# Value products alone in their PSUM banks, global scores in one bank, and new orders of loads, of ScalarE and of the end, in an attention and soft-MoE kernel

## Chip, cores and metric
One core of one Trainium2 chip, all data fp32 (the mask constants are bf16). The time is device microseconds of one execution. The change is judged by the ratio of the times of the two kernels.

## Reference
Attention over 8 batches and 8 heads with 512 local and 32 global tokens, head size 64. A local query sees the 32 global keys and the local keys at a distance of at most 32; a global query sees all 544. The result is a matrix of 4608 tokens x 512, which goes through a soft mixture of 8 experts with 4 slots each:

```python
s_g = scale * np.matmul(q_g, k_all.transpose(0, 1, 3, 2))
out_g = np.matmul(sm(s_g), v_all)
s_ll = np.where(mask, scale * np.matmul(q_l, k_l.transpose(0, 1, 3, 2)), -1000000000.0)
s_lg = scale * np.matmul(q_l, k_g.transpose(0, 1, 3, 2))
out_l = np.matmul(sm(np.concatenate([s_lg, s_ll], axis=-1)), np.concatenate([v_g, v_l], axis=2))
...
logits = x @ phi                          # 4608 x 512 by 512 x 32
d = softmax of logits over the tokens;  slot_input = d.T @ x
h = np.maximum(slot_input[e] @ w1[e], 0.0);  slot_out[e] = h @ w2[e]
c = softmax of logits over the slots;   return c @ slot_out
```

## The kernel before, in words
The attention runs in 32 steps s, one for two heads of one batch: b = s // 4, q = s % 4. Two steps, an even and an odd one, are a pair i = s // 2; the global queries of a pair are worked on together.

What one step does, engine by engine. TensorE forms the masked scores of the next step in tile pS (`scores`, 72 products); VectorE takes their maximum (L242) and subtracts it into the step's tile w (L244); TensorE turns w into pT (`turn_pair`, L120); ScalarE takes the exponentials of pT (L251); TensorE forms the value products of the step before in pO (`values`); VectorE normalises them into x (`normalise`, L286 to L288). GpSimd copies v into two shifted forms (L260 to L263).

Even steps also form the global scores of the pair: `global_small` in pT and `global_main` in both halves of pM, pM0 and pM1, one row half of 64 in each. ScalarE copies them to sgr in four copies of 64 partitions (L302, L312). VectorE takes the maximum gm (L319), GpSimd subtracts it into sgs (L322). TensorE turns sgs into columns of pO behind the value products (from column GOFF on), a part in the odd step (`turn_global(0)`) and a part in the next even step; ScalarE takes their exponentials into eg (L343). `global_values` forms the global outputs in pM1, and VectorE and GpSimd scale and place them (L360 to L366).

At odd steps the x of two steps is turned into both halves of pM and copied out as xT (L388). At q = 2 the logits of the batch before are formed in pM0, at q = 3 their running soft maximum follows (`soft`), the weights dT are turned into columns of pO and copied as dd (L349), and at q = 0 `sums` adds the weighted tokens to acc. Logits of the global tokens have a column of their own and extra steps (18 to 23).

Every engine runs its instructions in the order in which the code states them. SP issues all loads in the order of the list `queue` (L170): "k" is a load of q and k of a step (kq, 624 KB, 3 buffers), "v" its values (390 KB, 5 buffers), "p" a page of 512 KB of the experts' weights. `pump` paces a load by making it wait for a product of TensorE; `allowed` holds it back in the code until the step that frees its buffer has been written.

After the last step the logits of the last batch, the slot inputs and their sums follow. Then `first_product` (w1) of two groups of experts, each followed by `hidden` (relu and turning on TensorE and ScalarE), `combine_weights` for three groups of tokens (soft maximum over the slots on VectorE, L680 to L686), `second_product` (w2) for two halves of the columns, and `combine` for 9 groups of tokens per half, with copies to ob by VectorE (L725) and ScalarE (L726) and the DMA of the result.

PSUM is four tiles of two banks, pS, pT, pO and pM, for the whole program.

Of the kernel before, what the change touches and what calls it, by code (L numbers as in the profile page):

```python
# [7 lines left out]
F32 = mybir.dt.float32  # L8
# [25 lines left out]
GOFF = 4 * VD  # L34
# [24 lines left out]
def kernel(ctx, tc, kq, vS, phi, w1, w2, cst, cbf, out):  # L59
# [24 lines left out]
    lT = keep.tile([P, 9, P], F32, name="lT")  # L84
    acc = keep.tile([P, DM], F32, tag="acc", name="acc")
    xgs = [keep.tile([P, DM], F32, tag=f"xg{i}", name=f"xg{i}") for i in range(2)]
    mrun = keep.tile([P, 1], F32, name="mrun")
    lrun = keep.tile([P, 1], F32, name="lrun")
    wrm = keep.tile([P, 256], BF16, name="wrm")
    dT = keep.tile([P, P], F32, name="dT")  # L90
    dTg = keep.tile([P, P], F32, name="dTg")
    dd = keep.tile([P, P], F32, name="dd")
    ddg = keep.tile([P, 2 * NS], F32, name="ddg")
# [172 lines left out]
    xs = {}  # L266
# [12 lines left out]

    def normalise(s):  # L280
        b, p = s // 4, s % 4
        if p == 0:
            xs[b] = xp.tile([P, 4, DM], F32, tag="x", name=f"x{b}")
        r = xp.tile([P, 8], F32, tag="r", name=f"r{s}")
# [9 lines left out]
    def global_small(i):  # L294
        for pp in range(2):
            k = kqs[2 * i + pp]
            for h in range(2):
                o = pT[64 * h + 32 * pp:64 * h + 32 * pp + 32, h, 0:64]
                for n, sl in ((0, GCOPY), (1, 5)):
                    mm(o[:, 32 * n:32 * n + 32], k[HALF[h], SQG, :], k[HALF[h], sl, :])  # L300
        for h in range(2):
            nc.scalar.copy(at_cols(sgr, HALF[h], 96, [(384, 2), (1, 32)]),  # L302
                           pT[HALF[h], h, 0:64].rearrange("p (a j) -> p a j", a=2))

    def global_main(i):
        for pp in range(2):
            k = kqs[2 * i + pp]
            for h in range(2):
                o = (pM0, pM1)[h][64 * h + 32 * pp:64 * h + 32 * pp + 32, 0:480]
                mm(o, k[HALF[h], SQG, :], at_cols(k, HALF[h], 0, [(192, 3), (32, 5), (1, 32)]))  # L310
        for h in range(2):
            nc.scalar.copy(at_cols(sgr, HALF[h], 0, [(32, 3), (P, 5), (1, 32)]),  # L312
                           (pM0, pM1)[h][HALF[h], 0:480].rearrange("p (r m j) -> p r m j", r=3, m=5))
# [3 lines left out]
    def global_max(i):  # L317
        gm[i] = xp.tile([P, 1], F32, tag="gm", name=f"gm{i}")
        nc.vector.reduce_max(gm[i], sgr, axis=AX.X)  # L319

    def global_shift(i):
        nc.gpsimd.tensor_scalar(sgs, sgr, gm[i], None, ALU.subtract)  # L322

    def turn_global(n):
        a, b = [], []
        for u, m in enumerate((0, 1, 2) if n == 0 else (3, 5)):
            lo, w = (P * m, 96 if m == 3 else P) if m < 4 else (480, P)
            src = sgs[:, lo:lo + w]
# [3 lines left out]
        return a, b  # L332

    def spare(u, n, w=P):

        return pO[0:w, :, GOFF + 64 * u:GOFF + 64 * (u + n)].rearrange("p r (u q) -> p u r q", q=64)

    def split(ap):
        return ap.rearrange("p u (r q) -> p u r q", r=2)

    def exp_global(n):
        for m, u, k, w in (((0, 0, 3, P),) if n == 0 else ((3, 0, 1, 96), (4, 1, 1, P))):
            nc.scalar.activation(split(eg[0:w, m:m + k, :]), spare(u, k, w), AF.Exp, scale=SCALE)  # L343

    def turn_d(src):
        return turn(lambda rt: pO[:, rt, GOFF + P:GOFF + 192], src)

    def copy_d():
        nc.scalar.copy(split(dd.unsqueeze(1)), spare(2, 1))  # L349
# [483 lines left out]
```

## Time and profile before
| | |
|---|---|
| time, median of 3 runs | 441.36 us (437.74 to 445.11) |
| the profiled execution, its own time | 442.88 us |
| its span | 441.1 us |
| TensorE busy, matmul | 271.7 us (62%) |
| VectorE, ScalarE, GpSimd busy | 173.3, 111.8, 130.7 us |
| mean granted clock of TensorE | 0.79 |
| moved by DMA | 77.10 MB, mean 175 GB/s |

The granted clock is given as a share of 2.4 GHz, so that 0.50 is the lower of the two levels. The chain that ended last is the list of what held up the end, followed back from the last instruction. An engine that is idle away from this chain costs nothing.

### The profile page before, as it was taken

To read this page: it belongs to the slowest core of one execution; us is meant where nothing else is said; L and a number is where in the kernel's file an instruction comes from. 1 tells how busy PE (TensorE), PEld (TensorE's weight loads), DVE (VectorE), ACT (ScalarE), POOL (GpSimd) and SP (SyncE) were. 2 spreads that over 40 slices of the span, in tenths; PEclk is the share of its full clock that TensorE was granted. 3 is DMA by queue.
4 is the path that set the end of the run, shared out by engine and by line. 5 is a ranking of instruction groups with operands and counts; after the bars stand their busy time and mean duration, and the time that the engine had idled before them with its cause. 6 is when DMAs were issued, how large, how long until landed. Compare 5 with 4: busy or idle time off the path is not lost.

```text
span 441.1 us, 15926 instructions
## 1 busy us (share of the span) xinstructions
PE 271.7 (62%) x7283; PEld 183.8 (42%) x7283; DVE 173.3 (39%) x329; ACT 111.8 (25%) x253; POOL 130.7 (30%) x216
## 2 busy tenths in 40 slices
PE   6673854555574657376566646457657686477852
PEld 4553634443453544355444434346445332243320
DVE  2544625352435434343534326254552322413231
ACT  1322413321322222233322213133251201212231
POOL 2536334260436143414251315143540000000000
PEclk9858869695969677868776859597995699589955
DMA  7655463425445253535353154444434989404774
GB/s 279 228 195 181 146 249 124 166 60 216 120 181 198 91 175 114 175 113 182 108 170 93 53 174 155 180 155 173 145 147 135 400 317 393 186 2 157 247 241 166
DMA packets 27907, 77.10 MB, mean 175 GB/s; under 512 B 2368, under 2 KB 11456, under 8 KB 27840
## 3 DMA queue, kind: packets, MB, share of 16 engines
q1 hardware_dynamic: 27840, 76.08, 49.0%
q8 instruction: 57, 0.93, 0.8%
q14 instruction: 10, 0.08, 0.1%
HBM read 67.16 MB, written 8.91 MB: 172 GB/s over the span
## 4 chain that ended last, share of the span: by engine, by line
PE 41%; DMA 20%; DVE 13%; ACT 6%; issue 4%; SPq 2%; POOL 1%; DVEq 0%; ACTq 0%
DMA kq<-in_kq_dram 20%; PE pS L117 16%; PE pO L117 8%; PE pM L117 8%; PE pT L117 4%; PE pM L120 2%; DVE ob L725 2%; ACT eg L343 2%; DVE x L288 2%; PE pT L120 2%; DVE mx L242 1%; PE pO L120 1%; SPq L154 1%; DVE w L244 1%; ACT sgr L312 1%
## 5 line engine op out<-in xcount | busy, mean ns | idle before, releaser
L242 DVE TENSOR_REDUCE mx<-pS 128x8 f32<-128x1024 f32 x32 | 39.2, 1224 | 116.1 <-PE pS L117 115.8
L117 PE MATMUL pO<-v,w 128*32 128x65 f32 x768 | 42.0, 245 | 48.4 <-ACT eg L343 38.4
L322 POOL TENSOR_SCALAR sgs<-sgr,gm 128x608 f32<-128x608 f32 x16 | 28.9, 1805 | 120.3 <-DVE gm L319 111.3
L117 PEld LDWEIGHTS pO<-v,w 128*32 128x32 f32 x768 | 36.2, 124 | 53.1 <-ACT eg L343 41.9
L117 PE MATMUL pS<-kq 64*32 64x128 f32 x2048 | 51.5, 340 | 0.7 <-issue 0.5
L117 PE MATMUL pT<-kq 64*32 64x32 f32 x256 | 12.3, 223 | 61.1 <-DMA kq<-in_kq_dram 61.1
L117 PEld LDWEIGHTS pS<-kq 64*32 64x32 f32 x2048 | 45.9, 130 | 3.7 <-issue 1.4
L251 ACT ACTIVATE w<-pT 128x1024 f32<-128x1024 f32 x32 | 32.7, 1023 | 44.3 <-PE pO L120 38.2
L117 PE MATMUL pO<-va,w 128*32 128x65 f32 x768 | 42.0, 244 | 0.0
L117 PE MATMUL pO<-vb,w 128*32 128x65 f32 x512 | 41.2, 244 | 0.0
L260 POOL COPY va<-v 128x650 f32<-128x650 f32 x32 | 23.2, 726 | 56.3 <-issue 48.0
L244 DVE TENSOR_TENSOR w<-pS,mx 128x1024 f32<-128x1024 f32 x32 | 39.2, 1224 | 1.1
L117 PEld LDWEIGHTS pO<-va,w 128*32 128x32 f32 x768 | 36.2, 125 | 0.0
L117 PEld LDWEIGHTS pT<-kq 64*32 64x32 f32 x256 | 8.5, 129 | 66.4 <-DMA kq<-in_kq_dram 63.0
L117 PEld LDWEIGHTS pO<-vb,w 128*32 128x32 f32 x512 | 35.3, 125 | 0.0
L120 PE MATMUL pT<-con,w 64*128 64x64 f32 x512 | 31.7, 248 | 0.0
L312 ACT COPY sgr<-pM 64x480 f32<-64x480 f32 x32 | 17.7, 554 | 48.4 <-PE pM L117 48.1
L117 PE MATMUL pM<-kq 64*32 64x480 f32 x128 | 28.6, 891 | 0.0
L302 ACT COPY sgr<-pT 64x64 f32<-64x64 f32 x32 | 6.6, 207 | 82.8 <-PE pT L117 78.4
L120 PEld LDWEIGHTS pT<-con,w 64*128 64x128 f32 x512 | 27.1, 160 | 1.3 <-issue 1.3
L120 PEld LDWEIGHTS pO<-con,sgs 64*128 64x128 f32 (+1 forms) x160 | 16.5, 152 | 26.5 <-DVE mx L242 15.4
L286 DVE TENSOR_SCALAR r<-pO 128x8 f32<-128x8 f32 x32 | 5.3, 167 | 52.9 <-PE pO L117 52.9
(156 smaller groups left out, 509.9 us busy)
## 6 DMA issues: line engine op xcount, KB each, us to landing
w<-in_w_dram SPq DMA_DIRECT2D x60, 512.0 KB, 5.8
kq<-in_kq_dram SPq DMA_DIRECT2D x32, 624.0 KB, 4.7
v<-in_vS_dram SPq DMA_DIRECT2D x32, 390.0 KB, 3.5
out_dram<-ob SPq DMA_DIRECT2D x16, 512.0 KB, 4.0
xw<-in_w_dram SPq DMA_DIRECT2D x4, 512.0 KB, 4.7
out_dram<-ob SPq DMA_DIRECT2D x4, 128.0 KB
cb<-in_cbf_dram SPq DMA_DIRECT2D x1, 176.0 KB, 2.4
con<-in_cst_dram SPq DMA_DIRECT2D x1, 130.0 KB, 5.1
```

What stands on the lines that cost most here:

```text
L117: return counted(2 if l.dtype == BF16 else 4, nc.tensor.matmul(o, l, r, start=start, stop=stop))
L120: return counted(2, nc.tensor.transpose(o, src, idn))
L242: nc.vector.reduce_max(mx, g, axis=AX.X)
L244: nc.vector.tensor_tensor(ws[s], g, bc(mx, P), ALU.subtract)
L251: nc.scalar.activation(ws[s], pT.rearrange("p r (u q) -> p (r u q)", q=64), AF.Exp, scale=SCALE)
L260: nc.gpsimd.tensor_copy(va, v[:, 0:5])
L288: nc.vector.tensor_tensor(xs[b][:, :, P * p:P * p + P].rearrange("p t (h d) -> p h t d", h=2), o[:, :, :, 0:D], bc(r.rearrange("p (h t) -> ...
L302: nc.scalar.copy(at_cols(sgr, HALF[h], 96, [(384, 2), (1, 32)]), pT[HALF[h], h, 0:64].rearrange("p (a j) -> p a j", a=2))
L312: nc.scalar.copy(at_cols(sgr, HALF[h], 0, [(32, 3), (P, 5), (1, 32)]), (pM0, pM1)[h][HALF[h], 0:480].rearrange("p (r m j) -> p r m j", r=3 ...
L322: nc.gpsimd.tensor_scalar(sgs, sgr, gm[i], None, ALU.subtract)
L343: nc.scalar.activation(split(eg[0:w, m:m + k, :]), spare(u, k, w), AF.Exp, scale=SCALE)
L725: nc.vector.tensor_copy(o[:, 0:2, :], pS[:, :, c])
```

## The change
The loads: in `queue` the two kq of a pair stand together, then a page, then the two v of the same pair instead of the next one, then a page.

The banks: pO holds value products alone. The turned global scores and the turned dT go to columns 256 to 511 of both halves of pM, behind the turned tokens, of which each step now turns one set of four (`turn_tokens(s - 2)`). All main global scores lie in pM0 (four products of 480 columns in four quarters of the partitions) and the small ones in pM1; they stand ahead of the scores of the next step, and ScalarE copies them with two instructions of 128 partitions.

The engines: the shift of the global scores goes from GpSimd to ScalarE as an Identity with bias (VectorE gives the maximum negated), the guard that `normalise` adds goes from VectorE to ScalarE (`guarded`), and so does the scaling of the global output. Exponentials stand behind `guarded` in ScalarE's order. Logits come at q = 1, the soft maximum at q = 2 and 3, sums at q = 3; the global logits become 32 further columns for batches 4 and 7.

The end: all combine weights are formed on VectorE ahead of the first `hidden`, a quarter of the second product's first half stands ahead of `hidden(1)`, the second half stands behind all combines of the first, and `combine` takes its banks in turn from pS, pT and pM, its copies in turn on ScalarE and VectorE.

```diff
     queue = [("k", 0), ("k", 1), ("v", 0), ("k", 2), ("v", 1), ("v", 2), ("p", 0), ("v", 3), ("p", 0), ("v", 4), ("p", 0)]
     for s in range(3, NP, 2):
-        queue += [("k", s), ("p", 0)] + ([("k", s + 1)] if s + 1 < NP else [])
-        queue += [("v", v) for v in (s + 2, s + 3) if v < NP]
+        queue += [("k", s)] + ([("k", s + 1)] if s + 1 < NP else []) + [("p", 0)]
+        queue += [("v", v) for v in (s, s + 1) if 5 <= v < NP]
         queue += [("p", 0)]
...
+    def guarded(s):
+        rs_[s] = xp.tile([P, 8], F32, tag="r", name=f"r{s}")
+        o = pO[:, :, 0:4 * VD].rearrange("p h (t d) -> p h t d", t=4)
+        nc.scalar.activation(rs_[s].rearrange("p (h t) -> p h t", h=2), o[:, :, :, D], AF.Identity, bias=guard)
+
...
-        o = pO[:, :, 0:GOFF].rearrange("p h (t d) -> p h t d", t=4)
-        nc.vector.tensor_scalar_add(r.rearrange("p (h t) -> p h t", h=2), o[:, :, :, D], GUARD)
+        r = rs_.pop(s)
+        o = pO[:, :, 0:4 * VD].rearrange("p h (t d) -> p h t d", t=4)
         nc.vector.reciprocal(r, r)
         nc.vector.tensor_tensor(
-            xs[b][:, :, P * p:P * p + P].rearrange("p t (h d) -> p h t d", h=2),
-            o[:, :, :, 0:D],
+            xs[b][:, :, P * p:P * p + P].rearrange("p t (h d) -> p h t d", h=2), o[:, :, :, 0:D],
             bc(r.rearrange("p (h t) -> p h t", h=2), D), ALU.mult)
...
-    def global_small(i):
+    def global_scores(i):
         for pp in range(2):
             k = kqs[2 * i + pp]
             for h in range(2):
...
-    def global_main(i):
+                R = slice(64 * h + 32 * pp, 64 * h + 32 * pp + 32)
+                mm(pM0[R, 0:480], k[HALF[h], SQG, :], at_cols(k, HALF[h], 0, [(192, 3), (32, 5), (1, 32)]))
         for pp in range(2):
             k = kqs[2 * i + pp]
             for h in range(2):
-                o = (pM0, pM1)[h][64 * h + 32 * pp:64 * h + 32 * pp + 32, 0:480]
-                mm(o, k[HALF[h], SQG, :], at_cols(k, HALF[h], 0, [(192, 3), (32, 5), (1, 32)]))
-        for h in range(2):
-            nc.scalar.copy(at_cols(sgr, HALF[h], 0, [(32, 3), (P, 5), (1, 32)]),
-                           (pM0, pM1)[h][HALF[h], 0:480].rearrange("p (r m j) -> p r m j", r=3, m=5))
+                R = slice(64 * h + 32 * pp, 64 * h + 32 * pp + 32)
+                for n, sl in ((0, GCOPY), (1, 5)):
+                    mm(pM1[R, 32 * n:32 * n + 32], k[HALF[h], SQG, :], k[HALF[h], sl, :])
+        nc.scalar.copy(at_cols(sgr, FULL, 0, [(32, 3), (P, 5), (1, 32)]),
+                       pM0[:, 0:480].rearrange("p (r m j) -> p r m j", r=3, m=5))
+        nc.scalar.copy(at_cols(sgr, FULL, 96, [(384, 2), (1, 32)]),
+                       pM1[:, 0:64].rearrange("p (a j) -> p a j", a=2))
...
         gm[i] = xp.tile([P, 1], F32, tag="gm", name=f"gm{i}")
-        nc.vector.reduce_max(gm[i], sgr, axis=AX.X)
+        nc.vector.tensor_reduce(gm[i], sgr, axis=AX.X, op=ALU.max, negate=True)
 
     def global_shift(i):
-        nc.gpsimd.tensor_scalar(sgs, sgr, gm[i], None, ALU.subtract)
+        nc.scalar.activation(sgs, sgr, AF.Identity, bias=gm[i])
+
+
+    def turned(c, n, w=P):
+        return pM[0:w, :, c:c + 64 * n].rearrange("p r (u q) -> p u r q", q=64)
...
+    def turn_to(c, src, w=P):
+        return turn(lambda rt: pM[0:w, rt, c:c + 64], src)
+    CG, CD = 256, 448
 
     def turn_global(n):
-        a, b = [], []
+        units = []
         for u, m in enumerate((0, 1, 2) if n == 0 else (3, 5)):
             lo, w = (P * m, 96 if m == 3 else P) if m < 4 else (480, P)
-            src = sgs[:, lo:lo + w]
-            x = turn(lambda rt, u=u, w=w: pO[0:w, rt, GOFF + 64 * u:GOFF + 64 * u + 64], src)
-            a.append(x[0])
-            b.append(x[1])
...
+            units.append(turn_to(CG + 64 * u, sgs[:, lo:lo + w], w))
+        return both(units)
     def exp_global(n):
         for m, u, k, w in (((0, 0, 3, P),) if n == 0 else ((3, 0, 1, 96), (4, 1, 1, P))):
-            nc.scalar.activation(split(eg[0:w, m:m + k, :]), spare(u, k, w), AF.Exp, scale=SCALE)
-    def turn_d(src):
+            nc.scalar.activation(split(eg[0:w, m:m + k, :]), turned(CG + 64 * u, k, w), AF.Exp, scale=SCALE)
...
-    def global_out(i, bank):
+    def global_out(i, bank, spread=False):
         b, g = i // 2, i % 2
         r = xp.tile([P, 1], F32, tag="rg", name=f"rg{i}")
         nc.vector.tensor_scalar_add(r, bank[:, D:D + 1], GUARD)
         nc.vector.reciprocal(r, r)
         og = xp.tile([P, D], F32, tag="og", name=f"og{i}")
-        nc.vector.tensor_tensor(og, bank[:, 0:D], r.broadcast_to([P, D]), ALU.mult)
+        nc.scalar.mul(og, bank[:, 0:D], r)
...
+    def step(s):
+
         ev, i, b, q = s % 2 == 0, s // 2, s // 4, s % 4
-        make_v(s)
-
-        if ev:
+        if s < NP:
+            make_v(s)
+        if ev and s < NP:
             need(kqs, s + 1, "k")
-            global_small(i)
+            global_scores(i)
         if s + 1 < NP:
             scores(s + 1)
-        if ev:
-            global_main(i)
         now["a"] = s
         if s + 1 < NP:
             shift(s + 1)
-        if ev:
-            global_max(i)
+        if q == 2 and s >= 6:
+            soft(b - 1, lT[:, b - 1, 0:LW if b - 1 in TOK else P])
+
+        ta, tb = turn_pair(s) if s < NP else ([], [])
+        if s >= 2:
+            xa, xb = turn_tokens(s - 2)
+            ta, tb = ta + xa, tb + xb
+        g = (1 if i >= 1 else None) if ev else 0
+        if g is not None:
+            xa, xb = turn_global(g)
+            ta, tb = ta + xa, tb + xb
         if q == 3 and b >= 1:
-            soft(b - 1, FULL, lT[:, b - 1, :], dT)
...
+            xa, xb = turn_to(CD, dT[:, 0:P])
+            ta, tb = ta + [xa], tb + [xb]
+        h0 = {18: 0, 20: 2}.get(s)
+        if h0 is not None:
+            xa, xb = turn_xg(0, CG + P, h0, h0 + 2)
+            ta, tb = ta + xa, tb + xb
+        run_pairs(ta, tb)
+        if g is not None:
+            exp_global(g)
+        if s >= 2:
+            copy_tokens(s - 2)
+        if q == 3 and b >= 1:
+            nc.scalar.copy(split(dd.unsqueeze(1)), turned(CD, 1))
+        if h0 is not None:
+            nc.scalar.copy(split(xTg[0][:, h0:h0 + 2, :]), turned(CG + P, 2))
 
         if s >= 1:
             values(s - 1)
+            guarded(s - 1)
+        if s < NP:
+            exps(s)
+        if q == 2 and s >= 6:
+            soft_exp(b - 1, lT[:, b - 1, 0:LW if b - 1 in TOK else P])
         if ev and i >= 1:
...
+            global_values(i - 1, pM1 if s < NP else pS[:, 1, :])
+        if q == 1 and b >= 1:
+            logits(b - 1, pM0)
+            if b - 1 in TOK:
+                logits_g(TOK[b - 1], pM0)
+        if q == 3 and b >= 1:
+            sums(b - 1, pM0)
         if s >= 1:
             normalise(s - 1)
         if ev and i >= 1:
-            global_out(i - 1, pM1)
-        if q == 2 and b >= 1:
...
+            global_out(i - 1, pM1 if s < NP else pS[:, 1, :], s == NP)
+        if q == 2 and s >= 6:
+            totals(b - 1)
+        if ev and s < NP:
+            global_max(i)
+            global_shift(i)
+        if q == 1 and b >= 1:
+            w = LW if b - 1 in TOK else P
+            nc.scalar.copy(lT[:, b - 1, 0:w], pM0[:, 0:w])
+        if q == 3 and b >= 1:
+            add_sums(b - 1, pM0)
         now["c"] = s
 
-
-    s = NP
+    for s in range(NP):
+        step(s)
+
...
-    def combine_weights(g):
+    def weights(g, bank):
+        n = 16 if g < 2 else 2
...
+    def turn_weights(g, bank):
+        lv = lvs[g]
+        if g < 2:
+            cTs[g] = xp.tile([P, 4, P], F32, tag="xT", name=f"cT{g}", bufs=4)
+            for k in range(4):
+                tr(bank[:, P * k:P * k + P], lv[:, 4 * k:4 * k + 4, :].rearrange("p t s -> p (t s)"), ident)
+            nc.scalar.copy(cTs[g], bank.rearrange("p (k q) -> p k q", k=4))
+        else:
+            cTs[g] = keep.tile([2 * NS, 1, P], F32, name="cTg")
+            tr(bank[0:2 * NS, 0:P], lv.rearrange("p t s -> p (t s)"), ident)
+            nc.scalar.copy(cTs[g][:, 0, :], bank[0:2 * NS, 0:P])
 
...
         cs = slice(256 * h, 256 * h + 256)
...
+        for t0 in range(0, 4 if b < B else 2, 2):
+            bank = (pS, pT, pM)[turn_no[0] % 3]
+            for t in (t0, t0 + 1):
+                R = slice(32 * t, 32 * t + 32)
+                mm(bank[:, t - t0, 0:256], cTs[b // 4][R, b % 4, :], sa[R, h, :])
+            (nc.vector.tensor_copy if turn_no[0] % 2 else nc.scalar.copy)(o[:, t0:t0 + 2, :], bank[:, :, 0:256])
+            turn_no[0] += 1
...
+    turn_logits(0, pM0)
+    turn_logits(1, pM1)
+    first_product(0, pO)
...
-    hidden(0, pT)
+    weights(0, pM0)
+    weights(1, pM1)
+    weights(2, None)
+    turn_weights(0, pT[:, 0, :])
+    turn_weights(1, pT[:, 1, :])
+    hidden(0, pO)
+    turn_weights(2, pT[:, 0, :])
     first_product(1, pS)
...
-    combine_weights(0)
+    second_product(0, 0, 4)
     hidden(1, pS)
-    combine_weights(1)
-    second_product(0, 0, 8)
-    combine_weights(2)
-    second_product(0, 8, 16)
+    second_product(0, 4, 16)
...
     slot_outputs(0)
     for b in range(B + 1):
         combine(0, b)
-        if b < 8:
-            second_product(1, b, b + 1)
-    second_product(1, 8, 16)
+    second_product(1, 0, 16)
```

SP's own order, at the loads for steps 19 to 22: kq, v and w (pages) with the program's numbers. Before:

```order
L154 DMA v19_2852<-in_vS_dram 128x780
L154 DMA v20_2854<-in_vS_dram 128x780
L146 DMA w18_2856<-in_w1_dram 128x1024
L150 DMA kq19_2897<-in_kq_dram 128x1248
L146 DMA w19_2941<-in_w1_dram 128x1024
L150 DMA kq20_2943<-in_kq_dram 128x1248
L154 DMA v21_3124<-in_vS_dram 128x780
L154 DMA v22_3126<-in_vS_dram 128x780
L146 DMA w20_3128<-in_w1_dram 128x1024
L150 DMA kq21_3237<-in_kq_dram 128x1248
```

After, the loads for steps 17 to 20:

```order
L150 DMA kq17_2337<-in_kq_dram 128x1248
L150 DMA kq18_2339<-in_kq_dram 128x1248
L146 DMA w17_2448<-in_w1_dram 128x1024
L154 DMA v17_2450<-in_vS_dram 128x780
L154 DMA v18_2543<-in_vS_dram 128x780
L146 DMA w18_2545<-in_w1_dram 128x1024
L150 DMA kq19_2718<-in_kq_dram 128x1248
L150 DMA kq20_2720<-in_kq_dram 128x1248
L146 DMA w19_2832<-in_w1_dram 128x1024
L154 DMA v19_2834<-in_vS_dram 128x780
L154 DMA v20_2919<-in_vS_dram 128x780
```

Before, kq21 stands behind v21, v22 and a page, and its pair mate kq20 on the other side of the two v. Now both kq of a pair stand together, and the v behind them are those of the same pair.

ScalarE's order from the global scores of an even step until the next step's tokens. sgr holds the copied global scores, eg the exponentials of the turned ones, w the local ones, xT the turned tokens, dd the turned weights. Before:

```order
L302 COPY sgr<-pT 64x2x32 x2
L312 COPY sgr<-pM 64x3x5x32 x2
L343 ACTIVATE eg<-pO 96x128
L343 ACTIVATE eg<-pO 128x128
L349 COPY dd<-pO 128x128
L251 ACTIVATE w_2491<-pT 128x1024
L251 ACTIVATE w_2653<-pT 128x1024
L343 ACTIVATE eg<-pO 128x384
L388 COPY xT_2844<-pM 128x512
L388 COPY xT_2846<-pM 128x512
```

After, the same stretch of a pair with logits (lT is their copy, of the turned global tokens first and then of the logits; r the guarded sums, og the scaled global output):

```order
L309 COPY sgr<-pM 128x3x5x32
L311 COPY sgr<-pM 128x2x32
L347 ACTIVATE eg<-pM 96x128
L347 ACTIVATE eg<-pM 128x128
L375 COPY xT_3308<-pM 128x512
L501 COPY lT<-pM 128x256
L283 ACTIVATE r_3347<-pO,guard 128x8
L251 ACTIVATE w_3126<-pT 128x1024
L361 ACTIVATE og_3375<-pM,rg_3372 128x64
L321 ACTIVATE sgs<-sgr,gm_3381 128x608
L347 ACTIVATE eg<-pM 128x384
L375 COPY xT_3469<-pM 128x512
```

The exponentials of w now stand behind the value products of the step before (r is read from them), and the new shift (sgs) stands behind those and ahead of the global exponentials and the copy of the tokens.

VectorE's order behind the slot inputs: rte is the factor that `hidden` needs, hs its output, cm and lv belong to the combine weights. Before:

```order
L647 TENSOR_SCALAR rte<-con,rt 128x2
L662 TENSOR_SCALAR hs_5364<-pT,rte 128x512 x2
L680 TENSOR_REDUCE cm_5434<-pM 128x16
L681 TENSOR_TENSOR lv_5432<-pM,cm_5434 128x512
L683 TENSOR_REDUCE cm_5434<-lv_5432 128x16
L684 TENSOR_SCALAR cm_5434<-cm_5434 128x16
L685 RECIPROCAL cm_5434<-cm_5434 128x16
L686 TENSOR_TENSOR lv_5432<-lv_5432,cm_5434 128x512
L662 TENSOR_SCALAR hs_5447<-pS,rte 128x512 x2
```

After:

```order
L613 TENSOR_SCALAR rte<-con,rt 128x2
L652 TENSOR_REDUCE cm_5340<-pM 128x16
L653 TENSOR_TENSOR lv_5339<-pM,cm_5340 128x512
L655 TENSOR_REDUCE cm_5340<-lv_5339 128x16
L656 TENSOR_SCALAR cm_5340<-cm_5340 128x16
L657 RECIPROCAL cm_5340<-cm_5340 128x16
L658 TENSOR_TENSOR lv_5339<-lv_5339,cm_5340 128x512
...
L628 TENSOR_SCALAR hs_5380<-pO,rte 128x512 x2
```

The factor is followed by three groups of combine weights (the first is shown), and the hidden rows come behind them; before, the hidden rows of the first product came first.

## Rows read from the trace of the kernel before

**Rows 1.** The page: chain that ended last, share of the span by engine.

```profile
PE 41%; DMA 20%; DVE 13%; ACT 6%; issue 4%; SPq 2%; POOL 1%; DVEq 0%; ACTq 0%
```

**Rows 2.** Waits: engine, tile, line, released by; us in total, times, longest us.

```profile
PE pT L117 <- DMA kq<-in_kq_dram: 61.1, 16, 7.8
...
PE pO L117 <- ACT eg L343: 38.4, 23, 3.7
```

**Rows 3.** Chain that ended last, in order of time, attention: start us, us, what.

```profile
49.65 1.12 PE pO L117 x64
...
149.38 0.75 PE pT L120 x14
...
150.84 1.16 PE pO L117 x64
...
153.87 1.08 PE pM L117 x32
154.95 1.33 PE pS L117 x71
...
162.40 3.86 DMA kq<-in_kq_dram
...
166.73 2.12 PE pS L117 x53
...
202.59 7.11 DMA kq<-in_kq_dram
...
262.87 1.01 PE pM L117 x8
...
321.47 1.11 PE pO L117 x64
```

**Rows 4.** Timeline of SP's DMA queue: start us, us, queue, line, what.

```profile
200.67 1.40 SPq L154 DMA_DIRECT2D v<-in_vS_dram  x2
...
202.12 0.42 SPq L146 DMA_DIRECT2D w<-in_w_dram  x1
```

**Rows 5.** Groups of instructions: busy us, mean ns of one, idle before.

```profile
L251 ACT ACTIVATE w<-pT 128x1024 f32<-128x1024 f32 x32 | 32.7, 1023 | 44.3 <-PE pO L120 38.2 <-issue 6.0
...
L288 DVE TENSOR_TENSOR x<-pO,r 128x512 f32<-128x512 f32 x32 | 22.1, 691 | 1.1
...
L388 ACT COPY xT<-pM 128x512 f32<-128x512 f32 x32 | 17.3, 598 | 8.3 <-PE pM L120 8.3
...
L319 DVE TENSOR_REDUCE gm<-sgr 128x1 f32<-128x608 f32 x16 | 12.5, 782 | 3.1 <-ACT sgr L312 3.1
...
L410 ACT ACTIVATE al<-mrun,nm 128x1 f32<-128x1 f32 x6 | 1.8, 294 | 20.9 <-DVE nm L408 20.9
```

**Rows 6.** Windows: length; busy PE, PEld, DVE, ACT, POOL; clock, DMA share, GB/s.

```profile
180.40:189.20 8.80, 0.98 (x60) 0.78 (x48) 1.06 (x3) 0.53 (x2) 2.67 (x4) 0.74 0.65 223
...
186.00:187.00 1.00, 0.00 (x0) 0.00 (x0) 0.00 (x0) 0.00 (x0) 0.00 (x0) 0.50 0.92 382
...
364.00:376.00 12.00, 7.82 (x70) 2.55 (x67) 3.52 (x7) 1.20 (x2) 0.00 (x0) 0.99 1.02 395
404.00:412.00 8.00, 6.83 (x88) 2.35 (x80) 3.93 (x6) 3.40 (x6) 0.00 (x0) 1.00 0.99 339
```

**Rows 7.** Chain that ended last, in order of time, the end: start us, us, what.

```profile
353.50 5.36 PE pT L117 x48
...
363.94 7.00 PE pS L117 x64
...
371.64 0.70 DVE cm L680
...
375.72 1.13 PE pM L120 x4
...
412.81 3.63 PE pO L117 x64
...
418.91 0.70 DVE ob L725
```

More of the change, by code (lines that the diff above doesn't have):

```diff
@@ new lines, in logits_g, with soft @@
+    def logits_g(i, bank):
+        for hc in range(4):
+            for t in range(4):
+                mm(bank[32 * t:32 * t + 32, P:LW], phisb[:, hc, :], xTg[i][:, hc, 32 * t:32 * t + 32], hc == 0, hc == 3)
+    st = {}
+    def soft(b, src):
+        w = LW if b in TOK else P
+        bm, rs = (xp.tile([P, 1], F32, tag=n, name=f"{n}{b}") for n in ("bm", "rs"))
+        nm = xp.tile([P, 1], F32, tag="nm", name=f"nm{b}", bufs=3)
+        if b == 0:
+            nc.vector.tensor_reduce(nm, src, axis=AX.X, op=ALU.max, negate=True)
+        else:
+            nc.vector.tensor_reduce(bm, src, axis=AX.X, op=ALU.max, negate=True)
+            nc.vector.tensor_tensor(nm, bm, st["nm"], ALU.min)
+        st.update({"old": st.get("nm"), "nm": nm, ("rs", b): rs})
@@ L414, in soft, with soft_exp, totals @@
+    def soft_exp(b, src):
+        w = LW if b in TOK else P
+        nm, rs = st["nm"], st["rs", b]
+        nc.scalar.activation(dT[:, 0:w], src, AF.Exp, bias=nm, accum_out=rs)
+        al = None
+        if b:
+            al = xp.tile([P, 1], F32, tag="al", name=f"al{b}", bufs=3)
+            nc.scalar.activation(al, st["old"], AF.Exp, bias=nm, scale=-1.0)
+        st["al", b] = al
+    def totals(b):
+        rs, al = st["rs", b], st["al", b]
+        if b == 0:
             nc.vector.tensor_copy(lrun, rs)
@@ L429, with add_sums @@
-    FULL, G3 = slice(0, P), slice(96, 128)
+            mm(out_[32 * t:32 * t + 32], dd[:, 32 * t:32 * t + 32], xs[b][:, t, c], True, b not in TOK)
+        if b in TOK:
+            for t in range(4):
+                R = slice(32 * t, 32 * t + 32)
+                mm(out_[R], de[R], xgs[TOK[b]][R, c], False, True)
+    def add_sums(b, src, c=slice(0, DM)):
+        if b == 0:
+            nc.vector.tensor_copy(acc[:, c], src)
+        else:
+            nc.vector.scalar_tensor_tensor(acc[:, c], acc[:, c], st["al", b], src, ALU.mult, ALU.add)
@@ L442 @@
     nc.gpsimd.memset(eg, 0.0)
-    nc.gpsimd.memset(dTg, 0.0)
-    nc.gpsimd.memset(lT[:, 8, :], 0.0)
+    nc.vector.memset(guard, GUARD)
     npe[0] = 48
@@ L578 @@
     new_pages(wC, 7)
[L580 to L581 removed]
+    xa, xb = turn_tokens(NP - 1)
+    ga, gb = turn_xg(1, CG, 0, 4)
     run_pairs(xa + ga, xb + gb)
[L583 to L586 removed]
+    copy_tokens(NP - 1)
+    nc.vector.tensor_copy(split(xTg[1]), turned(CG, 4))
     logits(B - 1, pl, 3, 4)
[L588 to L589 removed]
+    logits_g(1, pl)
     small = lambda n, w=1: keep.tile([P, w], F32, name=n)
[L593 removed]
     wq, wl, rt, rte, wm = small("wq"), small("wl"), small("rt"), small("rte", 2), small("wm", NS)
[L595 removed]
     mrow = keep.tile([1, 1, NS], F32, name="mrow")
@@ L598 @@
     sT = [keep.tile([P, 2, NS], F32, name=f"sT{i}") for i in range(2)]
[L599 to L607 removed]
+    soft(B - 1, pl[:, 0:LW])
+    soft_exp(B - 1, pl[:, 0:LW])
+    nm = st["nm"]
+    mt = pS[0:1, 1, 0:P]
     nc.tensor.transpose(mt, nm, ident)
```

276 lines of the change are left out of this document (67 added, 209 removed).

## The prediction
> **What bounds the kernel now.** I read the chain that ended last first. By engine it is 41% TensorE and 20% DMA [rows 1]; the DMA part is one transfer, kq, and TensorE's waits for it add up to 61.1 us in 16 waits, one per pair of steps, the longest 7.8 [rows 2]. The chain in order of time shows the form [rows 3]: values of an even step at 49.65 and again at 321.47 are 13 pairs apart, so a pair takes 271.8/13 = 20.9 us. Inside a pair stands a kq wait (3.86 us at 162.40, 7.11 at 202.59), and the scores behind it took 2.12 us (166.73) where those of the other step took 1.33 (154.95). The windows say why [rows 6]: with TensorE idle in that wait the granted clock was 0.50, the 1.2 GHz level. So a wait costs its own length and then 1.6 times the price of the work behind it.
>
> Why kq comes late is read from SP's queue [rows 4]: at 200.67 two v loads were issued, at 202.12 a page, and only then kq21, whose transfer the chain shows from 202.59 for 7.11 us [rows 3]. Its buffer was that of kq18, last read by the global scores of that step, which end ahead of the step's values; the two v loads in front of it wait for buffers of their own, which come free only behind those values. The load is late because of its place, not because the DMA engines are full.
>
> The second item is TensorE's wait for ACT's global exponentials, 38.4 us in 23 waits [rows 2]: the turned global scores lie in the banks of the value products, so these cannot start before ACT has read the scores away.
>
> **The change, part by part.** *Loads.* The two kq of a pair now go first, then a page, then the v of this pair. Each is paced on an instruction of TensorE two steps earlier, so kq(2i+1) goes out about 1.8 us before to 0.3 us after the end of the values of an even step and is wanted 6.9 us (the global scores) after it. Alone it needs about 3.9 us, behind v and a page 7.1 [rows 3]. It lands at 4 to 5 in the first case, hidden behind a chain that takes until 6.65 anyway; in the second it is up to 1 us late. I take the first. A pair moves 2 kq, 2 v and 2 pages = 3.05 MB: at the 395 GB/s of the input stage [rows 6] that is 7.7 us, under the pair's length.
>
> *Bounding chain without the loads.* I walked the new orders with the durations of the trace at the high clock, zero at the end of an even step's values. ACT: guard with a bias 0.29, exponentials 1.02; VectorE at the same time: a reciprocal, the multiply 0.69, two small ones of the global output, the maximum of the global scores 0.78 [rows 5]; with 0.2 to 0.3 for each small one and two handovers to ACT it ends at 2.54. Then the shift of the global scores, moved from GpSimd to ACT: the trace has no ACT operation of 128x608, but 128x512 takes 0.60 and 128x1024 1.02 [rows 5], so 0.68 by a straight line, 0.6 and 1.0 as bounds; I take 0.7 with its handover, ending at 3.35. TensorE has by then done the next scores (1.33), the pair turns (0.75) and token turns; it turns the global scores by 3.65 and does values (1.16) by 4.86, waits for ACT's copy of the tokens (0.60, hidden), logits 1.08 by 5.98 [rows 3, 5]. The next global scores need the bank that ACT empties: guard, exponentials and copy of the logits end at 6.6. From there global scores 1.0 and 0.3, scores 1.33, turns about 1.3, values 1.16 and 0.1 [rows 3]: 5.15. So 11.8 us for this pair. In the other kind of pair the soft maximum and the turned weights stand in place of the logits: ACT's copy of the weights ends at 6.0, the sums take about what the logits take, 1.1, and VectorE's accumulation about what the multiply takes, so that with handovers it ends at 8.05, so 8.15 + 5.15 = 13.3. Mean 12.55, of which TensorE is busy 10.6.
>
> *Edits that cost nothing.* The guard (VectorE to ACT) and the product of the global output (VectorE to ACT) are counted in this chain; the copy with 128 rows in place of two of 64 saves ACT some 0.5 us per pair under TensorE's scores. If that cover were gone it would be 0.5 us per pair, 8 us. Turning the global scores into spare columns of the token bank removes the wait of [rows 2]: late next is the shift on ACT, already in the walk. Queued behind ACT's shift are the global exponentials and the token copy, for which the logits wait; this is priced above.
>
> *A new risk of the global scores.* Both row halves now write one bank; before, each half had its own. Four products run at a time, in 1.0 us for 480 columns [rows 3]. If the halves are taken one after the other, 2.0. No row of before shows it, since there two row halves never meet in a bank; bounds 0 and +1.0 us per pair. I take 0, since the four outputs still have partitions of their own, and give the other a chance. The Trainium skill (PSUM — Partial Sum Buffer, section "PSUM bank collisions raise a hardware error") speaks against this edit: different row tiles cannot use the same bank at the same time and software has to see to it. By that rule the sum would be the 328 of the second rival.
>
> *The sum for attention.* 13 pairs at 20.9 - 12.55 = 8.35: 108.6 less. The two pairs ahead of 49.65 had their loads partly in place already; I credit 3 us each, 6. So values(29), which ended at 322.6, end at 208. From there to the first product at 353.50 [rows 7] before took 30.9; sums of one batch move ahead, and the values and logits there would run at the higher level, for which I take 8 (a choice; bounds 0 and 12): 23.
>
> *The end.* Before, first product at 353.50, the second at 363.94 for 7.00 [rows 7]. Now the combine weights of all groups stand on VectorE between them. One group took from 371.64 to 375.72, 4.1 us [rows 7]; two of these and a small one (2.1) after the denominators push the second product from 10.4 behind the first to 18.9: 8.5 us lost. Given back: between the second product's end (370.94) and the first copy of the second half (418.91) lay 48.0 us [rows 7], with three of those groups in it. Now it holds four terms of the second product's sum (0.45 each, since eight took 3.63 at 412.81 [rows 7]), the rest of the hidden turn 1.35, twelve more 5.4, slots 1.7, then nine combines at 0.75 (the copies of 0.7 now alternate on two engines) and sixteen terms: 14.1, slots and copies 3.2; together 27.6, 20.4 less. The last half from 418.91 to the end took 22.2; 4.46 MB at the output rate of 339 GB/s [rows 6] are 13.1, plus 4 until the last has landed (as a kq alone): 17.1, 5.1 less. Net 17 less. Bounds: 0 if VectorE's weights are not hidden under the first product's second part (8.5 more) and the outputs keep their pace, and 24.
>
> *Allowance.* 4% of the chain are handovers between engines [rows 1], 18 us. My walk has few of them; I add 8 (bounds 0 and 18).
>
> *Total*, against the profiled execution's own 442.88 us (span 441.1 and 1.8 around it; 1.5 above the median of 441.36): 442.9 - 114.6 - 7.9 - 17 + 8 = **311.4, say 312**.
>
> **The rivals.**
> 1. *The loads still hold the pair.* For: in the stretch around the worst wait DMA moved 223 GB/s [rows 6]; at that rate a pair's 3.05 MB take 13.7 us and, with kq queued behind v of the pair before, TensorE would wait some 1.5 us per pair. Against: 395 GB/s in the page stage. 15 x 1.5 = 24: 336.
> 2. *Row halves in one bank follow each other:* 16 x 1.0: 328.
> 3. *The clock stays at its lower level for half the pairs.* For: the 3.86 us wait was enough to bring scores of 2.12 [rows 3]. Against: the walk has no single wait over about 1.5 us, and with short ones the trace shows scores of 1.33. TensorE's 10.6 us become 17 and with the waits 19 per pair; half of 15 x 6.5 is 49: 361. The Trainium skill (TensorE: Matmul & The Clock Gate, section "HAM oscillation — how this bites in real kernels") describes this: waits for DMA in a loop that put each turn of it back at the low clock. Before agrees, with 2.12 behind each kq wait.
> 4. *The other side: lower level throughout.* If ACT's longer list (shift, guard, product and copies) puts waits into every step that keep the clock at 0.50, a pair takes 20 us, 15 x 7.5 = 112 more, and the end some 26 more: 450. It decides against the change from about nine tenths of attention at the lower level. TensorE alone holds 17 of the 20, so little room is left before, and none of the waits in my walk is that long.
>
> **How the numbers follow.** Forecast 0.60 (its own range 296 to 325, from the bounds of attention's tail, the end and the handovers); loads 0.15 (325 to 345), one-bank products 0.07 (325 to 335); half at the lower clock 0.11 (345 to 380); gain eaten to within 2% 0.04; slower 0.03. Range 296 to 352: it leaves out the worse part of the third rival and what lies below. Within 2% is about what a measurement of this kernel can tell from no change. Faster 0.93, same 0.04, slower 0.03.
>
> **What would show it.** Pair length 12 to 13.5 between the values of even steps; no kq row in the chain of waits beyond 10 us in all; scores of 1.33 in both steps and a granted clock near 1 through attention; global scores of 1.0 in both halves; ACT's shift near 0.7; second product 19 us behind the first, and about 28 between its end and the first copy of the second half. Wrong if kq waits stay over 20 us in all, if 2.12 us scores stay in every pair, or if ACT's line has become the longest idle reason of TensorE.

## The result

| | before | changed |
|---|---|---|
| median | 440.02 us (437.74 to 445.11, 4 runs) | 336.56 us (333.11 to 341.29, 4 runs) |
| ratio | | 0.7636 (95% interval 0.7546 to 0.7725) |
| profiled execution, its span | 442.88, 441.1 us | 336.67, 334.9 us |

Some executions of either kernel run some per cent longer at a lower granted clock; medians here and below are over all executions, ratios over the others alone.

The forecast was 312 us, the range 296 to 352. The direction and most of the gain are there (103 us of 128); the time lies 25 us above the forecast. The page of the changed kernel, the chain that ended last by engine and the line of the instruction queue (packets, MB, share of 16 engines):

```profile
PE 63%; issue 13%; DVE 11%; ACT 7%; DMA 2%; SPq 1%; DVEq 0%; POOLq 0%; POOL 0%; ACTq 0%
```

```profile
q8 instruction: 57, 0.93, 1.1%
```

The DMA share of the chain has gone from 20% [rows 1] to 2%. In its place "issue" has grown from 4% (18.6 us by the pieces of the chain) to 13% (42.3 us): time in which an engine waited for nothing that the profile shows. Pieces of over 0.3 us ahead of TensorE are 1.2 of the 18.6 us, and 35.9 of the 42.3. The waits (us in total, times, longest):

```profile
PE pS L117 <- issue: 15.8, 10, 2.7
...
PE pO L117 <- issue: 12.1, 10, 2.5
...
PE pM L117 <- DMA kq<-in_kq_dram: 5.4, 1, 5.4
```

One wait for kq is left, at the start, where there were 16 with 61.1 us [rows 2]; TensorE's wait for ScalarE's global exponentials is no longer in the list. The chain in order of time (start, us, what):

```profile
37.34 2.48 issue
40.40 1.05 PE pM L117 x12
41.62 2.13 PE pS L117 x59
...
47.45 2.66 issue
50.11 1.31 PE pS L117 x64
...
228.10 1.16 PE pM L117 x20
...
232.98 0.71 PE pO L117 x36
...
257.37 6.43 PE pO L117 x48
...
278.48 7.84 PE pS L117 x64
...
297.05 0.48 PE pS L117 x2
...
305.42 7.09 PE pO L117 x128
...
315.91 0.70 DVE ob L699
```

Global scores (pM) stand at 40.40 and at 228.10, 13 pairs apart: 14.44 us per pair, where it was 20.9 and 12.55 was forecast. Two groups of instructions more (busy us, mean ns, idle before), and the main global scores of one pair alone, those at 40.33 and, in the kernel before, those at 210.87:

```profile
L321 ACT ACTIVATE sgs<-sgr,gm 128x608 f32<-128x608 f32 x16 | 12.8, 802 | 8.7 <-DVE gm L318 8.7
...
L283 ACT ACTIVATE r<-pO,guard 128x8 f32<-128x8 f32 x32 | 8.6, 267 | 21.7 <-PE pO L117 19.4 <-PE pM L117 2.0
```

```profile
L117 PE MATMUL pM<-kq 64*32 64x480 f32 x8 | 1.0, 574 | 0.0
```

```profile
L117 PE MATMUL pM<-kq 64*32 64x480 f32 x8 | 1.1, 562 | 0.0
```

The shift took 0.80 (0.7 with its handover was put down), the guard 0.27 (0.29). These prices held within some 0.1 us.

**Where the gaps are.** The timeline of TensorE shows one in the middle of the value products, between two products that need nothing new:

```profile
150.79 0.22 PE L117 MATMUL pO<-v,w 128*32 128x65 f32 x1
153.50 0.22 PE L117 MATMUL pO<-va,w 128*32 128x65 f32 x1 [2.48 <-issue]
```

The ends of the gaps cut the program into windows; their columns are as in [rows 6], with the number of instructions of each engine in brackets:

```profile
39.85:50.12 10.27, 7.61 (x258) 5.79 (x259) 5.15 (x9) 5.06 (x11) 4.11 (x9) 0.83 0.72 237
50.12:58.97 8.85, 7.63 (x261) 6.20 (x261) 3.35 (x4) 2.98 (x7) 4.81 (x8) 0.81 0.70 227
58.97:63.06 4.09, 2.90 (x132) 2.47 (x132) 3.10 (x5) 2.06 (x6) 0.00 (x0) 1.00 0.81 271
63.06:67.88 4.82, 2.71 (x130) 2.22 (x130) 3.86 (x7) 1.52 (x5) 2.76 (x7) 1.00 0.78 259
67.88:80.59 12.71, 10.74 (x386) 7.58 (x386) 5.84 (x10) 5.96 (x14) 3.90 (x8) 0.87 0.44 146
80.59:85.42 4.83, 3.62 (x129) 2.92 (x130) 3.31 (x4) 2.39 (x5) 4.44 (x9) 1.00 0.90 265
```

Products and weight loads together are 517, 522, 264, 260, 772 and 259: two, two, one, one, three and one times 256, with a few counted on both sides of a cut. So TensorE stops at places that are 256 of its instructions apart, whatever stands there. The whole trace says the same: TensorE has 24 stops of over 0.3 us that the profile puts down to "issue", 35.4 us in all, and with its products and weight loads counted in order every one of them stands 65 to 73 instructions ahead of a multiple of 256. The page has 57 packets of 0.93 MB on the instruction queue, and TensorE has 7345 products and as many weight loads, 57.4 times 256. In each of the eight stops of 2 us and more such a packet starts within about 0.5 us of the stop's beginning. In the trace each of these packets takes 0.9 to 1.5 us and no two start less than 3.3 us apart in attention, while TensorE gets through the 144 instructions of a step's scores in some 1.3 us and the 128 of its values in 1.1 when nothing holds it. That is a theory of its own, and the experiments test it: **TensorE runs out of instructions** (A). Its rival (B): the gaps are handovers between engines or TensorE's own pace on the columns. A third (C): loads of data hold up the loads of instructions.

### The profile page after: what moved, and what is told of

It reads as the page before. It is cut to its first block, busy times and chain, and to the rows that moved or that the text cites. A ratio compares the mean times of both kernels' runs of the same rounds, so it can differ in the third digit from the quotient of the medians.

```text
span 334.9 us, 15942 instructions
## 1 busy us (share of the span) xinstructions
PE 244.9 (73%) x7345; PEld 166.7 (50%) x7345; DVE 158.0 (47%) x269; ACT 120.9 (36%) x279; POOL 100.8 (30%) x196
## 4 chain that ended last, share of the span: by engine, by line
PE 63%; issue 13%; DVE 11%; ACT 7%; DMA 2%; SPq 1%; DVEq 0%; POOLq 0%; POOL 0%; ACTq 0%
PE pS L117 18%; PE pO L117 17%; PE pM L117 14%; PE pT L120 6%; PE pM L120 6%; DMA kq<-in_kq_dram 2%; ACT w L251 2%; PE pM L446 2%; DVE acc L439 2%; DVE ob L699 1%; DVE x L292 1%; DVE mx L242 1%; DVE w L244 1%; PE pT L117 1%; ACT r L283 1%
## 5 line engine op out<-in xcount | busy, mean ns | idle before, releaser
L117 PE MATMUL pS<-kq 64*32 64x128 f32 x2048 | 43.1, 286 | 11.1 <-issue 11.1
L365 POOL COPY xg<-og 32x64 f32<-32x64 f32 x62 | 14.2, 229 | 107.5 <-ACT og L361 105.6
L117 PEld LDWEIGHTS pS<-kq 64*32 64x32 f32 x2048 | 36.9, 110 | 14.1 <-issue 13.3
L117 PEld LDWEIGHTS pO<-v,w 128*32 128x32 f32 x768 | 33.3, 116 | 7.2 <-issue 4.9
L347 ACT ACTIVATE eg<-pM 128x384 f32<-128x384 f32 (+2 forms) x48 | 14.9, 343 | 54.6 <-PE pM L120 54.6
L117 PE MATMUL pM<-kq 64*32 64x32 f32 (+1 forms) x384 | 23.5, 345 | 14.6 <-DMA kq<-in_kq_dram 5.4
L117 PEld LDWEIGHTS pM<-kq 64*32 64x32 f32 x384 | 9.2, 113 | 36.1 <-issue 11.0
L292 DVE TENSOR_TENSOR x<-pO,r 128x512 f32<-128x512 f32 x32 | 22.1, 692 | 3.3
L261 POOL COPY va<-v 32x650 f32<-32x650 f32 x32 | 23.0, 719 | 2.0
L117 PE MATMUL pS<-cb 64*32 64x512 bf16 x256 | 16.5, 412 | 8.3 <-issue 4.7
L309 ACT COPY sgr<-pM 128x480 f32<-128x480 f32 x16 | 8.9, 559 | 34.5 <-PE pM L117 34.4
```

The costliest lines, as they stand in the source:

```text
L117: return counted(2 if l.dtype == BF16 else 4, nc.tensor.matmul(o, l, r, start=start, stop=stop))
L261: nc.gpsimd.tensor_copy(va[0:32], v[0:32, 1:6])
L292: nc.vector.tensor_tensor(xs[b][:, :, P * p:P * p + P].rearrange("p t (h d) -> p h t d", h=2), o[:, :, :, 0:D], bc(r.rearrange("p (h t) -> ...
L309: nc.scalar.copy(at_cols(sgr, FULL, 0, [(32, 3), (P, 5), (1, 32)]), pM0[:, 0:480].rearrange("p (r m j) -> p r m j", r=3, m=5))
L347: nc.scalar.activation(split(eg[0:w, m:m + k, :]), turned(CG + 64 * u, k, w), AF.Exp, scale=SCALE)
L365: copy(xgs[b // 4][32 * (b % 4):32 * (b % 4) + 32, D * hd:D * hd + D], og[32 * j:32 * j + 32, :])
```

## The experiments

Each ratio is to the kernel before on the same chip.

**The base.** The changed kernel was run twice more beside the others.

> The changed kernel once more, beside the others of this set on the same chip. Both theories: 336 us as before, ratio to the kernel before 0.76; its chain of waits has about 43 us of 'issue' in the attention and the end, and this is the base for the other runs.

341.02 us, 5 us above what was expected, ratio 0.7733 (0.7637 to 0.783).

> The changed kernel as it is, as the base for the run with the new end on the same chip: 336 to 341 us, ratio 0.77.

340.79 us, ratio 0.7682 (0.761 to 0.7754). The three series agree within their intervals.

**The loads, taken out of the change.**

```diff
-        queue += [("k", s)] + ([("k", s + 1)] if s + 1 < NP else []) + [("p", 0)]
-        queue += [("v", v) for v in (s, s + 1) if 5 <= v < NP]
+        queue += [("k", s), ("p", 0)] + ([("k", s + 1)] if s + 1 < NP else [])
+        queue += [("v", v) for v in (s + 2, s + 3) if v < NP]
```

> The changed kernel with SP's old order of loads. Theory A (late kq was the bound, and its waits come back): TensorE's waits for kq rise from 5 us in one wait to 40 us or more, the time to 365 to 385 us, and the 'issue' part of the chain falls under 25 us, since instructions can be brought in while TensorE waits for kq. Theory B (the banks and the order of ScalarE carry the gain, the order of loads matters little): at most 345 us and under 10 us of kq waits.

400.79 us, ratio 0.9166 (0.9077 to 0.9254). Its waits and its chain:

```profile
PE pM L117 <- DMA kq<-in_kq_dram: 53.2, 15, 5.7
```

```profile
PE 43%; DMA 32%; DVE 8%; issue 6%; ACT 3%; SPq 2%; POOL 1%; POOLq 0%; DVEq 0%; ACTq 0%
```

The waits for kq are back and cost more than expected (401 against 365 to 385); 13 pairs take 19.1 us each (here and below from the third to the last maximum of the global scores in the timeline). Of all that the change does, this order is worth some 63 us (0.9166 less 0.7733 of the base run beside it, times 438). "issue" falls to 6% of 398 us, about 25 us, and TensorE's stops to 15 with 16.0 us. This fits the view that its instructions arrive while it waits for kq, and that the kernel before showed two such stops for this reason.

**The loads alone, put into the kernel before** (the same four lines the other way round), twice:

> The kernel before with only the new order of loads. Theory A: kq waits fall from 61 us to under 15, the pair is then held by the banks of the value products and the shift on GpSimd at some 16.5 us, time about 375 us (360 to 395). Theory B: the loads alone bring little, 420 us or more.

> The kernel before with only the new order of loads, once more for a profile: 372 to 378 us; kq waits under 10 us, TensorE's wait for ScalarE's global exponentials still near 38 us as in the kernel before, so that a pair takes some 17 us.

377.02 and 376.31 us, the second with ratio 0.8612 (0.8481 to 0.8742). Waits of the second run:

```profile
PE pO L117 <- ACT eg L343: 34.3, 23, 3.7
...
PEld pT L117 <- DMA kq<-in_kq_dram: 4.3, 2, 3.6
```

61 us of the 100 come from the order of loads alone, with nothing else changed. The wait for the global exponentials is still there (34.3, before 38.4 [rows 2]); 13 pairs take 16.3 us each. The banks and the new orders of the engines then bring them to 14.4, some 24 us, and the new end about 10; both are differences, and what the banks bring without the new orders was not run.

**The shift of the global scores back on GpSimd.**

```diff
-        nc.scalar.activation(sgs, sgr, AF.Identity, bias=gm[i])
+        nc.gpsimd.tensor_scalar(sgs, sgr, gm[i], None, ALU.add)
```

> The changed kernel with the shift of the global scores back on GpSimd (1.8 us there instead of 0.8 on ScalarE). If the pair is held by the chain of engines that was walked before the run: 1.0 us and a handover more for each of 16 pairs, 18 to 22 us, 355 us. If TensorE's supply of instructions sets the pair (256 at a time, 57 loads of 16 KB): most of it hides under stalls of that kind, 5 to 10 us more, 341 to 346 us, and 'issue' falls by about the same amount.

340.65 us, ratio 0.7772 (0.771 to 0.7834): no difference to the base, so less than either theory had said. The chain:

```profile
PE 55%; DVE 13%; issue 9%; ACT 9%; POOL 7%; DMA 3%; SPq 0%; POOLq 0%; DVEq 0%; ACTq 0%
```

GpSimd now holds 7% of the chain and "issue" has fallen from 12% in the base run of this set (41.8 us by its pieces) to 9% (31.7). Its pieces of over 0.3 us ahead of TensorE are 18.6 us here and 35.6 in the base run. By what the chain of engines gets longer, the gaps get shorter. So the chain that I had walked no longer sets the pair by itself, and this part of the change brings nothing that these runs can measure.

**Fewer instructions for the same columns.** Twice as wide products, half as many, in scores and values; what is computed is not the reference's.

```diff
-        for i in range(4):
+        for i in (0, 2):
...
-                    win = at_cols(k, HALF[h], 32 * a, [(32 * x, 2), (32 * y, 2), (1, 32)])
+                    win = at_cols(k, HALF[h], 32 * a, [(1, 256)])
...
-            for t in range(4):
+            for t in (0, 2):
...
-                mm(pO[32 * cc:32 * cc + 32, h, VD * t:VD * t + VD],
+                mm(pO[32 * cc:32 * cc + 32, h, VD * t:VD * t + 2 * VD],
...
-                       (vs, vas, vbs)[cls][s][:, m, h, :])
+                       (vs, vas, vbs)[cls][s][:, m, :, :])
```

> The changed kernel with half as many, twice as wide products in the local scores (256 columns instead of 128) and in the values (130 instead of 65): the same columns go through TensorE, with 128 instructions fewer per step, 4096 of 14690. The result is not the reference's. Theory A (TensorE runs out of instructions, which come in blocks of 256, at least 3.4 us apart in the trace of the changed kernel): 41 loads instead of 57, the 'issue' part of the chain falls from 41 us to under 18, the time to 300 to 312 us. Theory B (the gaps are handovers between engines, or TensorE's own pace on the columns): 'issue' stays above 30 us, the time between 325 and 340 us.

363.55 us, slower, and neither theory had said so. The chain:

```profile
PE 39%; DMA 32%; DVE 14%; ACT 4%; SPq 4%; issue 3%; POOL 0%; POOLq 0%; DVEq 0%; ACTq 0%
```

"issue" did fall, to 3%, but DMA rose to 32%. The experiment had moved a second thing: `pump` is called once per 256 instructions of TensorE that the code counts, so with fewer products each load was paced behind a later one. The run was made again with a wide product counted as two, in scores and values, which puts the loads at their old places:

```diff
-                       False, i == 2)
+                       False, i == 2, n=8)
```

> The run with fewer, wider products again, with the loads now paced at the same places of the program as in the changed kernel: the pacing counts products, and half of these were gone in the first try, so that its loads went out late (kq is 29% of its chain). The result is not the reference's. Theory A (supply of instructions): kq waits under 12 us, 'issue' under 15 us, time 300 to 312 us. Theory B (handovers, TensorE's own pace): 'issue' over 30 us, 325 to 340 us.

300.87 us, ratio 0.6857 (0.6746 to 0.6969). The instruction queue, the head of the chain and the window of 13 pairs:

```profile
q8 instruction: 41, 0.67, 0.9%
```

```profile
PE 46%; DVE 28%; ACT 11%; issue 5%; DMA 5%; SPq 0%; DVEq 0%; ACTq 0%; POOLq 0%; POOL 0%
```

```profile
42.00:198.00 156.00, 132.34 (x3806) 88.25 (x3790) 104.67 (x173) 84.89 (x205) 80.68 (x156) 0.99 0.73 254
```

The same 13 pairs in the changed kernel:

```profile
40.00:230.00 190.00, 147.01 (x5547) 110.64 (x5541) 106.33 (x169) 85.69 (x204) 83.79 (x160) 0.93 0.66 216
```

34 us less. TensorE's busy time fell by 14.7, its idle time from 43.0 to 23.7, 19.3 us. Theory A had 300 to 312 us and "issue" under 15; it came out at 300.87 and 5%, 15.6 by its pieces. B had 325 to 340. The pair is at 12.0 us here, and VectorE holds 28% of the chain: this is near the pair that I had walked. The test is not quite clean, since fewer weight loads and the higher clock (0.99) also make TensorE's own work shorter; the idle time is the part that speaks for A. Put down to "issue" in these two windows are 33.3 us of TensorE's idle time in the changed kernel and 6.0 here; over the whole run the largest entry of this kind, 15.8 us in the changed kernel, is now

```profile
PE pS L117 <- issue: 3.2, 4, 1.4
```

**The pages later**, behind the last q, k and v:

```diff
+    queue = [q for q in queue if q[0] != "p"] + [q for q in queue if q[0] == "p"]
     queue += [("b", a) for a in (("a", 28), ("a", 30), ("a", 30), ("c", 30), ("c", 31))]
```

> The changed kernel with all pages of the experts' weights behind the last q, k and v in SP's order, so that attention moves 2.0 instead of 3.05 MB per pair. The whole time grows, since 27 pages then stand between attention and the experts (some 30 us); what is read is attention alone. Theory A (the supply of instructions has a pace of its own): 'issue' on TensorE in attention stays near 35 us, the pair at 14 to 15 us. Theory C (loads of data hold up the loads of instructions, or the DMA engines are full): 'issue' falls under 18 us and the pair to 12.5 to 13 us.

346.14 us (two runs). The window of attention:

```profile
40.00:228.00 188.00, 142.30 (x5474) 106.92 (x5470) 106.49 (x174) 85.74 (x206) 81.34 (x156) 0.95 0.47 157
```

The DMA engines are busy for 0.47 of it instead of 0.66, yet TensorE stands idle for 45.7 us (43.0 with the pages), 33.9 of them "issue" (33.3), and 13 pairs take 14.39 us each. C falls: the supply has a pace of its own, which less data does not quicken. The total grew by some 5 us only against the base of the same set (340.79), less than the 30 expected. Part of that is a quicker start: the third pair's maximum of the global scores stands at 40.9 us, in the changed kernel at 47.9; the rest was not looked into.

**A new end.** `hidden(0)` ahead of the combine weights, which then run on VectorE beside the second product; the turned logits go to pS and the second product to pT:

```diff
-    turn_logits(0, pM0)
-    turn_logits(1, pM1)
+    turn_logits(0, pS[:, 0, :])
+    turn_logits(1, pS[:, 1, :])
     first_product(0, pO)
...
-    weights(0, pM0)
-    weights(1, pM1)
-    weights(2, None)
-    turn_weights(0, pT[:, 0, :])
-    turn_weights(1, pT[:, 1, :])
     hidden(0, pO)
-    turn_weights(2, pT[:, 0, :])
-    first_product(1, pS)
+    weights(0, pS[:, 0, :])
+    weights(1, pS[:, 1, :])
+    first_product(1, pT)
...
-    second_product(0, 0, 4)
-    hidden(1, pS)
-    second_product(0, 4, 16)
+    second_product(0, 0, 8)
+    hidden(1, pT)
+    weights(2, None)
+    turn_weights(0, pS[:, 0, :])
+    turn_weights(1, pS[:, 1, :])
+    second_product(0, 8, 16)
+    turn_weights(2, pS[:, 0, :])
```

> The changed kernel with a new end: the first hidden rows are formed before the combine weights on VectorE, and the weights run beside the second product of w1. If the weights on VectorE between the two are what holds the end (first product to second 21 us in the changed kernel, 10.4 before): the second product starts 10 to 12 us behind the first, and the whole time falls by 6 to 10 us, to about 329 us. If the weights only come to stand elsewhere on the path: within 2 us of the changed kernel.

328.80 us, ratio 0.7475 (0.7436 to 0.7513), against 0.7682 (0.761 to 0.7754) for the changed kernel on the same chip: this version beats both. Its chain:

```profile
255.00 6.01 PE pO L117 x48
...
266.04 7.00 PE pT L117 x64
```

The second product starts 11.0 us behind the first (21.1 in the changed kernel), and from the first product to the end are 68.6 us instead of 77.5. The 8.9 us stand where they were expected, and they are the whole gain: the ratios differ by 0.0207, of 437 us 9.0.

**The stops, counted.** TensorE's idle times of over 0.3 us that the profile puts down to "issue", in the profiled execution of each run:

| run | stops | us in all |
|---|---|---|
| before | 2 | 1.2 |
| before, with the new loads (second run) | 12 | 14.3 |
| changed | 24 | 35.4 |
| changed, once more (first base run) | 28 | 38.0 |
| changed, old loads | 15 | 16.0 |
| changed, shift on GpSimd | 24 | 28.1 |
| changed, pages late | 26 | 37.0 |
| changed, fewer instructions, paced | 7 | 5.9 |

They grow as other waits go, shrink as a wait is put back or the instructions become fewer, and do not care for the pages.

## Why the prediction was right, and where it was off

The late kq: right. It was the first thing to be read in the chain, and the runs on the order of loads give it 61 and 63 us (the four lines move v as well as kq, and the two were not taken apart). Behind the first two pairs no wait for kq is left, although I had given 0.15 to the case that loads still hold the pair. That rival's 336 us is what was measured, but by another mechanism: kq waits of 5.4 us, not 24. So there is luck in the range: the forecast's own bounds ended at 325, and the 337 us lie in 296 to 352 only because rivals that did not come true had widened it.

The walk of the pair: its prices held within some 0.1 us (shift, guard, global scores). The main global scores at 40.33 are eight product records; they take 1.01 us in one bank, and so in 11 of the 16 pairs, where in two banks they had taken 1.14 at the higher clock level (at 210.87 before). So the row halves do not follow each other, and that rival falls. The Trainium skill's rule (PSUM — Partial Sum Buffer, section "PSUM bank collisions raise a hardware error") that different row tiles cannot use a bank at the same time costs no time here, with these 1.01 us, where the outputs lie on different partitions. The granted clock rose to 0.93 over 13 pairs (0.79 over the same pairs before), so both rivals on the clock fall; single steps at the lower level remain, as the scores of 2.13 at 41.62 show.

The step that failed is the **allowance**: "4% of the chain are handovers between engines [rows 1], 18 us. My walk has few of them; I add 8". As a reading of the kernel before this holds: of its 18.6 us of "issue" TensorE's stops are 1.2. For handovers the 8 us were enough too: without TensorE's stops the changed kernel's chain has 6.4 us of "issue". What the sum left out is a term that this row did not show, the supply of TensorE's instructions. I put it at nothing without a reason, and it measured 35.9 us of the chain. With all the waits of the kernel before TensorE stopped for 1.2 us, with the waits for kq alone put back for 16.0: they had been time in which instructions arrived. I had not asked what an engine does that waits for nothing the profile shows.

The pair is 14.44 instead of 12.55, 24.6 us over 13 pairs. Of the 1.89 us more, 1.3 is idle time of TensorE (43.0 us in 13.2 pairs, 3.27 each, where the walk has 1.95) and 0.6 is longer work (11.17 busy instead of 10.6), which goes with a granted clock of 0.93 where the walk took the higher level throughout. The stops are 2.5 of the 3.27, so in part they stand in the place of waits that had been walked.

The pieces then add up: values of step 29 end at 233.7 instead of 208 (25.7 more), from there to the first product 23.7 instead of 23, from there to the end 77.5 instead of 70.6, less the 8 us of the allowance: 25.3, and 311.4 + 25.3 is the profiled 336.7. Two sums of the prediction are off by little and change nothing: the 5.15 us of the walk are 5.19, and two kq, two v and two pages of 624, 390 and 512 KB (of 1024 bytes) are 3.13 MB, 7.9 us at 395 GB/s.

The Trainium skill (Runtime: NRT & Kernel Launch, section "Instruction fetch mechanics") has blocks of 16 KB, 256 instructions, which the trace confirms (57 packets, 0.93 MB, gaps 256 apart); it adds that crossing such a boundary is mostly hidden. Here the measurement decides: it was hidden in the kernel before (two stops, 1.2 us), and is not in this one (24 stops, 35.4 us).

The end: the sign was right, 10.1 us less (87.6 to 77.5) instead of 17. The 6.9 us between them lie all along it: the second product started 21.1 us behind the first (18.9 forecast), took 7.84 (7.00), from its end to the first copy of the second half at 315.91 passed 29.6 (27.6), and from there to the end 19.0 (17.1). That the weights on VectorE lose time between the two products was named in the prediction, and the run with the new end shows that it was worth changing.

ScalarE's edits: the prediction priced the shift on the path at 0.7 and had no answer to what it brings; the run with the shift on GpSimd shows nothing measurable, since gaps of the other kind take it up.

## What to carry to other kernels

When the largest wait of a chain is about to go, ask what used that wait for cover: a small "issue" share says how much of a supply was seen, not how much there is. Count the instructions of the densest engine between waits (an fp32 product is four of TensorE's here, two weight loads and two products) against the pace at which they come, before the chain of engines is walked. And an experiment that changes the number of instructions must keep whatever is paced by them.

## What was not expected of the hardware

In the changed kernel TensorE stops for 0.4 to 2.7 us at places 256 of its instructions apart. Loads of instructions start at least 3.3 us apart, which is at most 78 instructions per us, and take 0.9 to 1.5 us, with page loads in the background or without. Where stops stand at two neighbouring boundaries, the shortest times between their ends are 3.7 to 4.0 us (178.29 and 182.01, 94.21 and 98.21), 64 to 69 instructions per us; in other runs the shortest is 3.4. By this pace the 842 instructions of a pair (11088 in 13.2 pairs) would take 12.2 to 13.2 us, an estimate: about as long as the pair that was walked. So the 14.44 would come from supply and waits together, which is argued and not shown. Why loads are not asked for earlier stays open: no run here shows what triggers one.
